# Causal attention in pairs of heads: the last 64 keys of two q-tiles transposed as one block

## The chip, the cores and the metric

The kernel runs on one core of one Trainium2 chip. The metric is the device time of one execution in microseconds (us); of several runs the median counts.

## What is computed

Attention over 2 batches of 12 heads, 448 queries and keys of 64 numbers each, with a causal mask, and behind it two gated layers on the 896 tokens of width 768. All inputs are float32.

```
scores = q @ k.T / 8;  scores[key > query] = -1e9
attn   = exp(scores - rowmax);  attn /= attn.sum() + 1e-9
x      = (attn @ v), heads put side by side          # 896 x 768
x      = (sigmoid(x @ w_gate) * (x @ w_val)) @ w_out  # 768 -> 1536 -> 768
h      = x @ w_in
out    = (h * cos(h)) @ w_out2                        # 768 -> 2048 -> 768
```

## The kernel before

**Tiling.** Two heads of one batch make a pair; there are 12 pairs (t = 0 to 11). The 448 queries are cut into seven q-tiles of 64; the two heads of a pair stand one above the other, so that a q-tile fills 128 partitions. Under the causal mask q-tile i needs 64*(i+1) keys, so its row of probabilities is that wide: 64, 128, ... 448 columns. All seven rows of a pair lie in one buffer `pbuf` (three of them, in turn), at the columns `POFF`; a row with an odd number of 64s (i = 0, 2, 4, 6) has 64 zeros behind it, set once at the start, so that it can be cut into blocks of 128 keys.

**Stages of a pair.** `scores(t)` (L263) makes, tile by tile in the order `ORDER`, the products with the keys on TensorE (PE, L276), the row maximum on VectorE (DVE, L280), and exp with the row's sum on ScalarE (ACT, L284). `normalise(t)` (L255) adds 1e-9 to the sums on GpSimd (POOL, L257), takes the reciprocals on DVE (L258), and multiplies each row in place, rows 0 to 6 one after the other, on POOL (L261). `transposes(t)` (L292) turns 16 blocks of 128x128 on PE (L300), four to a PSUM bank, and copies the banks to `pt`, banks 0 and 2 on DVE (L306), banks 1 and 3 on ACT (L304). `attend(t)` (L309) multiplies with the values (L316): four key blocks j, and for each the q-tiles that need it, one matmul for each head; all fall on one bank. `split_x` takes the result out as a high part (ACT, L328) and a low one (DVE, L330).

**Order.** The schedule is written by hand: every engine runs its instructions in program order. An iteration t of the loop holds `scores(t)`, the loads for later pairs (on SP's queue), `attend(t - 2)`, and `transposes(t - 1)`. Inside the transposes, ahead of the copy of bank 3, stands `normalise(t)`: its reciprocal is queued on DVE behind the copy of bank 2, and the POOL rows of pair t follow that reciprocal. The pair t = 0 alone is normalised in three pieces (`FIRST_ROWS`). From t = 3 on, one step of the preparation of the first weights (`prepare`, lines L137 to L158, on ACT or DVE) stands at the end of each `scores(t)`.

**After attention.** The layers behind it are 2448 matmuls of 448 columns (L209 to L211), with weights that DVE and ACT decode from 64-bit words. The first fifteen and three more of them stand between `transposes(10)`, `attend(10)`, `transposes(11)` and `attend(11)`.

The blocks of the transposes are listed as (q-tile, key block of 128):

```
POFF = [0, 128, 256, 512, 768, 1152, 1536]
BLOCKS = (
    [(i, 0) for i in range(7)] + [(6, 3)]
    + [(i, 1) for i in range(2, 7)] + [(i, 2) for i in range(4, 7)]
)
```

Of the kernel before, what the change touches and what calls it, by code (L numbers as in the profile page):

```python
# [9 lines left out]
F32 = mybir.dt.float32  # L10
# [4 lines left out]
ALU = mybir.AluOpType  # L15
PSUM = bass.MemoryType.PSUM

P = 128
B, H, S, D = 2, 12, 448, 64
NPAIR = H // 2  # L20
# [12 lines left out]
WARM = 26  # L33


POFF = [0, 128, 256, 512, 768, 1152, 1536]
PW = 2048

BLOCKS = (
    [(i, 0) for i in range(7)] + [(6, 3)]  # L40
    + [(i, 1) for i in range(2, 7)] + [(i, 2) for i in range(4, 7)]
)

# [4 lines left out]
VOFF = NQT * QKW  # L50

FIRST_LOADS = ((0, 2), (2, 4), (4, 7))
ATW = VOFF + 4 * P

INV2PI = 1.0 / (2.0 * math.pi)

# [5 lines left out]
def attn_moe_moe2(  # L62
# [9 lines left out]
    nc = tc.nc  # L72
# [8 lines left out]
    def bank():  # L81
        return psum.tile([P, 512], F32, tag="ps", name="ps")
# [14 lines left out]
    for m in range(KX):  # L97
        for c in range(0, KG, WC):
            n = min(WC, KG - c)
# [114 lines left out]
    with tc.tile_pool(name="apool", bufs=1) as apool, tc.tile_pool(name="a2", bufs=2) as a2:  # L214
        ident = apool.tile([P, P], F32, name="ident")
        mask = apool.tile([P, S], F32, name="mask")
        pbuf = [apool.tile([P, PW], F32, name=f"pbuf{i}") for i in range(3)]

# [8 lines left out]
        def load_v(t):  # L227
            vs[t] = a2.tile([P, ATW - VOFF], F32, tag="v", name="v", bufs=4)
            nc.sync.dma_start(out=vs[t], in_=qkv[t, :, VOFF:])
# [15 lines left out]
                compare_op=ALU.is_ge, fill=-8.0e9, base=0, pattern=[[-1, D]], channel_multiplier=1,  # L245
            )
        make_identity(nc, ident)
        for pb in pbuf:
            for i in (0, 2, 4, 6):
                w = D * (i + 1)  # L250
                nc.gpsimd.memset(pb[:, POFF[i] + w : POFF[i] + w + D], 0.0)

        pts, soft = {}, {}

        def normalise(t, i0, i1):  # L255
            pb, (sums, rs) = pbuf[t % 3], soft[t]
            nc.gpsimd.tensor_scalar(sums[:, i0:i1], sums[:, i0:i1], 1e-9, 1.0, op0=ALU.add, op1=ALU.mult)  # L257
            nc.vector.reciprocal(rs[:, i0:i1], sums[:, i0:i1])  # L258
            for i in range(i0, i1):
                row = pb[:, POFF[i] : POFF[i] + D * (i + 1)]  # L260
                nc.gpsimd.tensor_scalar(row, row, rs[:, i : i + 1], 1.0, op0=ALU.mult, op1=ALU.mult)  # L261

        def scores(t):  # L263

            blocks = qk.pop(t).rearrange("p (n c) -> p n c", c=QKW)
            pb = pbuf[t % 3]
            nm = a2.tile([P, 8], F32, tag="nm", name="nm")
            sums = a2.tile([P, 8], F32, tag="sums", name="sums")
            soft[t] = sums, a2.tile([P, 8], F32, tag="rs", name="rs")
            for n, i in enumerate(ORDER):  # L270
                w = D * (i + 1)
                ps = bank()
                for h in range(2):
                    rows = slice(h * D, h * D + D)
                    o, k0 = ((1 - h) * D, 2 * D) if i in CROSSED else (h * D, D)
                    mm(  # L276
                        ps[o : o + D, :w], lhsT=blocks[rows, i, :D],
                        rhs=blocks[rows, : i + 1, k0 : k0 + D], start=True, stop=True,
                    )
                nc.vector.tensor_tensor_reduce(  # L280
                    out=ps[:, :w], in0=ps[:, :w], in1=mask[:, S - w :], scale=-0.125, scalar=3.0e38,
                    op0=ALU.add, op1=ALU.min, accum_out=nm[:, i : i + 1],
                )
                nc.scalar.activation(  # L284
                    pb[:, POFF[i] : POFF[i] + w], ps[:, :w], AF.Exp, scale=-1.0,
                    bias=nm[:, i : i + 1], accum_out=sums[:, i : i + 1],
                )
                if (t, n) in FIRST_ROWS:
                    normalise(0, *FIRST_ROWS[t, n])
            next(preparing, None)  # L290

        def transposes(t, before=lambda g: None):  # L292
            pb = pbuf[t % 3]
            pt = a2.tile([P, 16, P], F32, tag="pt", name="pt")
            for g in range(4):
                ps = bank()
                for s in range(4):
                    i, j = BLOCKS[4 * g + s]
                    c = POFF[i] + j * P
                    nc.tensor.transpose(ps[:, s * P : s * P + P], pb[:, c : c + P], ident)  # L300
                before(g)
                dst = pt[:, 4 * g : 4 * g + 4].rearrange("p a b -> p (a b)")
                if g % 2:
                    nc.scalar.copy(dst, ps)  # L304
                else:
                    nc.vector.tensor_copy(dst, ps)  # L306
            pts[t] = pt

        def attend(t):  # L309

            v, pt = vs.pop(t), pts.pop(t)
            ps = bank()
            for j, (s0, s1) in ((0, (0, 7)), (3, (7, 8)), (2, (13, 16)), (1, (8, 13))):
                for h in range(2):
                    v0 = j * P + h * D
                    mm(  # L316
                        ps[h * D : h * D + D, j * P : S],
                        lhsT=v[:, v0 : v0 + D],
                        rhs=pt[:, s0:s1, h * D : h * D + D],
                        start=j == 0, stop=j == 1,  # L320
                    )
            xps[t] = ps

# [137 lines left out]
    for m in range(KX):  # L461
        ps2 = [bank(), bank()]
        for c in range(nch):
# [4 lines left out]
            for b in range(B):  # L468
                products(ps2[b], wt, HG[c * WC : min(KG, c * WC + WC)], b, c == 0, c == nch - 1)
                if c == nch - 1:  # L470
                    o = tpool.tile([P, S], F32, tag="t0", name="o")
                    rows, c0 = slice(m * P, m * P + P), b * S
# [12 lines left out]
def _layouts(inputs):  # L485
    import numpy as np

    f = np.float32
    q = inputs["q"].reshape(B, NPAIR, 2, NQT, D, D)
    k = inputs["k"].reshape(B, NPAIR, 2, S, D)  # L490
    v = inputs["v"].reshape(B, NPAIR, 2, S, D)
    pk = np.zeros((B, NPAIR, P, ATW), f)
    kt = k.transpose(0, 1, 2, 4, 3)
    qt = q.transpose(0, 1, 2, 5, 3, 4).copy()
    for i in CROSSED:
        qt[:, :, :, :, i] = qt[:, :, ::-1, :, i].copy()
    vb = np.zeros((B, NPAIR, 4 * P, 2, D), f)
    vb[:, :, :S] = v.transpose(0, 1, 3, 2, 4)
    qk = pk[..., :VOFF].reshape(B, NPAIR, P, NQT, 3, D)
    for n, part in enumerate((qt, kt, kt[:, :, ::-1])):  # L500
        qk[..., n, :] = part.reshape(B, NPAIR, P, NQT, D)
    pk[..., :VOFF] = qk.reshape(B, NPAIR, P, VOFF)
    pk[..., VOFF:] = vb.reshape(B, NPAIR, 4, P, P).transpose(0, 1, 3, 2, 4).reshape(B, NPAIR, P, 4 * P)

    def blocks(w):
        w = np.ascontiguousarray(w).view(np.int64)
        kk, nn = w.shape
        return w.reshape(kk // P, P, nn // P, P).transpose(2, 1, 0, 3)

    gv = np.stack([blocks(inputs["moe_w_gate"]), blocks(inputs["moe_w_val"])], axis=2)  # L510
    return {
        "qkv": pk.reshape(B * NPAIR, P, ATW),
        "w_gv": gv,
        "w_out": blocks(inputs["moe_w_out"]),
        "w_in2": blocks(inputs["moe2_w_in"]),
        "w_out2": blocks(inputs["moe2_w_out"]),
    }
# [20 lines left out]
```

## Time and profile before

| | us |
|---|---|
| median of 3 runs (lowest, highest) | 585.95 (585.24, 587.32) |
| the profiled execution, its own time | 587.1 |
| span of the profiled execution | 585.0 |
| PE busy in the span | 578.9 (99%) |
| DVE busy | 377.1 (64%) |
| ACT busy | 273.3 (47%) |
| POOL busy | 45.7 (8%) |
| chain that ended last: PE / POOL | 98% / 1% |

The profile is of one execution; its span goes from the first to the last instruction and is 2.1 us shorter than that execution's own time. PE counts as busy from the start of a matmul to its modelled end, so that 99% does not say that it never waited; the chain of work that ended last, followed back from the last instruction, says more. POOL works in the first 75 us only. Attention takes the span up to about 79 us, with the layers' first products set in at its end.

### The profile page before, as it was taken

Reading aid. Unit: us, or ns where it says so; the run is one execution under the profiler, and the core shown is the slowest. Engines: PE = TensorE matmul, PEld = TensorE weight load, DVE = VectorE, ACT = ScalarE, POOL = GpSimd, SP = SyncE. Lnnn points to the kernel's source line nnn. Section 1 sums busy time; section 2 is a strip of 40 time slices with the busy share of each in tenths; the row PEclk is TensorE's granted clock in tenths of the full one; section 3 lists DMA queues with packets and bytes.
Section 4 is the critical chain, followed back from the end, with each engine's and each line's share of the span. In section 5 each row is a group of like instructions: output and inputs, shape, how many; then the busy total and the mean of one; then the engine's idle time right before and its main releaser. Section 6 shows DMA issues by size and latency. Waiting matters only on the chain.

```text
span 585.0 us, 8308 instructions
## 1 busy us (share of the span) xinstructions
PE 578.9 (99%) x3194; PEld 507.5 (87%) x3194; DVE 377.1 (64%) x659; ACT 273.3 (47%) x549; POOL 45.7 (8%) x119
## 2 busy tenths in 40 slices
PE   8999999999999999999999999999999999999997
PEld 5666789999999999999999999999999999999996
DVE  5899976666666666675555547888888866434620
ACT  6889753333333333332222228777777733312320
POOL 5656610000000000000000000000000000000000
PEclk9999999999999999999999999999999999999999
DMA  7755233333333333333333332333332334433300
GB/s 269 253 193 186 103 108 109 108 109 109 108 109 108 109 108 109 108 108 110 108 109 96 110 101 72 109 109 109 108 109 91 109 105 160 127 132 104 110 32 31
DMA packets 15734, 68.16 MB, mean 117 GB/s; under 512 B 1744, under 2 KB 3664, under 8 KB 15696
## 3 DMA queue, kind: packets, MB, share of 16 engines
q1 hardware_dynamic: 15408, 67.33, 35.5%
q8 instruction: 25, 0.41, 0.3%
q10 hardware_dynamic: 288, 0.31, 0.2%
q14 instruction: 13, 0.11, 0.1%
HBM read 64.88 MB, written 2.75 MB: 116 GB/s over the span
## 4 chain that ended last, share of the span: by engine, by line
PE 98%; POOL 1%; DVE 0%; issue 0%; ACT 0%; ACTq 0%
PE ps L210 29%; PE ps L209 29%; PE ps L211 29%; PE ps L316 4%; PE ps L300 4%; PE ps L276 3%; POOL pbuf L261 1%; PE ps L236 1%; DVE ps L280 0%; POOL sums L257 0%; DVE rs L258 0%; DVE o L476 0%; ACT o L475 0%; DVE nm L280 0%; DVE idle L233 0%
## 5 line engine op out<-in xcount | busy, mean ns | idle before, releaser
L209 PE MATMUL ps<-x,whi 128*128 128x448 f32 x480 | 176.9, 369 | 0.0
L210 PE MATMUL ps<-x,whi 128*128 128x448 f32 x480 | 176.6, 368 | 0.0
L211 PE MATMUL ps<-x,wlo 128*128 128x448 f32 x480 | 176.6, 368 | 0.0
L158 DVE TENSOR_TENSOR wlo<-wf,whi 128x768 fp32r<-128x768 f32 (+2 forms) x71 | 66.0, 930 | 94.6 <-ACT whi L156 92.5
L209 PE MATMUL ps<-h,whi 128*128 128x448 f32 x336 | 123.6, 368 | 0.0
L210 PE MATMUL ps<-h,whi 128*128 128x448 f32 x336 | 123.6, 368 | 0.0
L211 PE MATMUL ps<-h,wlo 128*128 128x448 f32 x336 | 123.6, 368 | 0.0
L209 PEld LDWEIGHTS ps<-x,whi 128*128 128x128 f32 x480 | 90.1, 188 | 9.5 <-issue 0.5
L210 PEld LDWEIGHTS ps<-x,whi 128*128 128x128 f32 x480 | 90.1, 188 | 9.1
L211 PEld LDWEIGHTS ps<-x,wlo 128*128 128x128 f32 x480 | 90.1, 188 | 9.0
L156 ACT ACTIVATE whi<-wf 128x768 fp32r<-128x768 f32 (+2 forms) x71 | 57.6, 812 | 42.7 <-DVE wf L147 42.7
L209 PEld LDWEIGHTS ps<-h,whi 128*128 128x128 f32 x336 | 63.1, 188 | 6.5
L211 PEld LDWEIGHTS ps<-h,wlo 128*128 128x128 f32 x336 | 63.1, 188 | 6.3
L210 PEld LDWEIGHTS ps<-h,whi 128*128 128x128 f32 x336 | 63.1, 188 | 6.3
L147 DVE SCALAR_TENSOR_TENSOR wf<-wraw,wf 128x768 uint32<-128x768 uint32 (+2 forms) x71 | 66.2, 932 | 2.4
L143 DVE SCALAR_TENSOR_TENSOR wf<-wraw,wf 128x768 uint32<-128x768 uint32 (+2 forms) x71 | 66.1, 931 | 2.4
L137 ACT ACTIVATE wf<-wraw 128x768 f32<-128x768 f32 (+2 forms) x71 | 61.8, 870 | 0.0
L385 ACT ACTIVATE h<-pr 128x448 fp32r<-128x448 f32 x24 | 13.9, 578 | 65.2 <-DVE pr L408 61.9
L284 ACT ACTIVATE pbuf<-ps,nm 128x64 f32<-128x64 f32 (+6 forms) x84 | 38.7, 479 | 8.5 <-DVE nm L280 7.5
L261 POOL TENSOR_SCALAR pbuf<-pbuf,rs 128x64 f32<-128x64 f32 (+6 forms) x84 | 40.1, 501 | 14.2 <-PE ps L276 9.2
L139 DVE TENSOR_SCALAR wf<-wf 128x768 uint32<-128x768 uint32 (+1 forms) x70 | 38.2, 546 | 1.3 <-ACT wf L137 0.7
L280 DVE CUSTOM_DVE_ANT_0 ps<-ps,mask 128x64 f32<-128x64 f32 (+6 forms) x84 | 32.9, 454 | 4.8 <-PE ps L276 4.6
(44 smaller groups left out, 404.3 us busy)
## 6 DMA issues: line engine op xcount, KB each, us to landing
wraw<-in_w_gv_dram SPq DMA_DIRECT2D x24, 768.0 KB, 4.3
wraw<-in_w_out_dram SPq DMA_DIRECT2D x24, 768.0 KB, 4.3
wraw<-in_w_in_dram SPq DMA_DIRECT2D x16, 768.0 KB, 4.3
qk<-in_qkv_dram SPq DMA_DIRECT2D x11, 672.0 KB, 4.2
v<-in_qkv_dram SPq DMA_DIRECT2D x12, 256.0 KB, 4.5
wraw<-in_w_out_dram SPq DMA_DIRECT2D x6, 512.0 KB, 3.8
out_dram<-o SPq DMA_DIRECT2D x11, 224.0 KB, 2.0
qk<-in_qkv_dram SPq DMA_DIRECT2D x1, 288.0 KB, 3.5
```

The source lines that it names most:

```text
L137: nc.scalar.activation(w, high.bitcast(F32), AF.Copy, scale=2.0**-112)
L139: nc.vector.tensor_scalar(bits, bits, 3, 0x7FFFFFFF, op0=ALU.logical_shift_left, op1=ALU.bitwise_and)
L143: nc.vector.scalar_tensor_tensor(bits, high, 0x80000000, bits, op0=ALU.bitwise_and, op1=ALU.bitwise_or)
L147: nc.vector.scalar_tensor_tensor(bits, low, 29, bits, op0=ALU.logical_shift_right, op1=ALU.bitwise_or)
L156: nc.scalar.activation(self.hi[:, e0:e1], self.w[:, e0:e1], AF.Copy)
L158: nc.vector.tensor_tensor(self.lo[:, e0:e1], self.w[:, e0:e1], self.hi.bitcast(F32)[:, e0:e1], op=ALU.subtract)
L209: mm(ps[:, :S], lhsT=hi[:, blk], rhs=r[:, 0, cols], start=first and k == 0, stop=False)
L210: mm(ps[:, :S], lhsT=hi[:, blk], rhs=r[:, 1, cols], start=False, stop=False)
L211: mm(ps[:, :S], lhsT=lo[:, blk], rhs=r[:, 0, cols], start=False, stop=last and k == n - 1)
L261: nc.gpsimd.tensor_scalar(row, row, rs[:, i : i + 1], 1.0, op0=ALU.mult, op1=ALU.mult)
L280: nc.vector.tensor_tensor_reduce(out=ps[:, :w], in0=ps[:, :w], in1=mask[:, S - w :], scale=-0.125, scalar=3.0e38, op0=ALU.add, op1=ALU.min ...
L284: nc.scalar.activation(pb[:, POFF[i] : POFF[i] + w], ps[:, :w], AF.Exp, scale=-1.0, bias=nm[:, i : i + 1], accum_out=sums[:, i : i + 1],)
```

## The change

The row of q-tile i no longer has zeros behind it. The half block that an odd row leaves over (its last 64 keys) is transposed together with that of another row: those of q-tiles 2 and 0 as one block, those of 6 and 4 as another. For that the rows stand in `pbuf` in another order: row 2 ends where row 0 begins, and behind row 6 there are 64 columns into which `normalise` writes the last 64 columns of row 4 (its first 256 stay in place). So POOL multiplies row 4 in two instructions, of 256 and of 64 columns. The memsets of the zeros are gone.

Of the 16 blocks 14 are left: six with j = 0 (q-tiles 1 to 6), the two mixed ones, four with j = 1, two with j = 2. The fourth bank holds two blocks, and its copy on ACT has 256 columns.

In `attend` a mixed block has two sorts of keys above each other, so the values come in seven blocks of 128 rows instead of four: three full ones, and four in which 64 rows are values and 64 are zeros. `VALUES` lists (values block, first slot, last slot, first q-tile); there are seven products for each head instead of four, over the same 16 tiles of 64 columns. The load of the values of a pair grows from 256 to 448 KB.

```diff
-POFF = [0, 128, 256, 512, 768, 1152, 1536]
-PW = 2048
+POFF = [192, 256, 0, 384, 1024, 640, 1344]
+APART = {4: 1792}
+HALF = {2: 128, 6: 1728}
+PW = 1856
 BLOCKS = (
-    [(i, 0) for i in range(7)] + [(6, 3)]
-    + [(i, 1) for i in range(2, 7)] + [(i, 2) for i in range(4, 7)]
+    [(i, 0) for i in range(1, 7)] + [(2, None), (6, None)]
+    + [(i, 1) for i in range(3, 7)] + [(i, 2) for i in (5, 6)]
 )
+VALUES = ((3, 6, 7, 0), (0, 0, 6, 1), (4, 6, 7, 2), (5, 7, 8, 4), (6, 7, 8, 6), (1, 8, 12, 3), (2, 12, 14, 5))
-ATW = VOFF + 4 * P
+NVB = 7
+ATW = VOFF + NVB * P
...
-        for pb in pbuf:
-            for i in (0, 2, 4, 6):
-                w = D * (i + 1)
-                nc.gpsimd.memset(pb[:, POFF[i] + w : POFF[i] + w + D], 0.0)
...
             for i in range(i0, i1):
-                row = pb[:, POFF[i] : POFF[i] + D * (i + 1)]
-                nc.gpsimd.tensor_scalar(row, row, rs[:, i : i + 1], 1.0, op0=ALU.mult, op1=ALU.mult)
+                c, w = POFF[i], D * (i + 1)
+                moves = [(c, c, w)]
+                if i in APART:
+                    moves = [(c, c, w - D), (APART[i], c + w - D, D)]
+                for c0, c1, w in moves:
+                    nc.gpsimd.tensor_scalar(
+                        pb[:, c0 : c0 + w], pb[:, c1 : c1 + w], rs[:, i : i + 1], 1.0,
+                        op0=ALU.mult, op1=ALU.mult,
+                    )
...
-                for s in range(4):
-                    i, j = BLOCKS[4 * g + s]
-                    c = POFF[i] + j * P
+                part = BLOCKS[4 * g : 4 * g + 4]
+                for s, (i, j) in enumerate(part):
+                    c = HALF[i] if j is None else POFF[i] + j * P
                     nc.tensor.transpose(ps[:, s * P : s * P + P], pb[:, c : c + P], ident)
...
-            for j, (s0, s1) in ((0, (0, 7)), (3, (7, 8)), (2, (13, 16)), (1, (8, 13))):
+            for j, s0, s1, i in VALUES:
                 for h in range(2):
                     v0 = j * P + h * D
                     mm(
-                        ps[h * D : h * D + D, j * P : S],
+                        ps[h * D : h * D + D, i * D : i * D + (s1 - s0) * D],
                         lhsT=v[:, v0 : v0 + D],
                         rhs=pt[:, s0:s1, h * D : h * D + D],
-                        start=j == 0, stop=j == 1,
+                        start=j in (0, 3), stop=j in (2, 3),
                     )
```

On PE, at the end of iteration 4 (`attend(2)`, then the transposes of pair 3), there stands before, with the waits of each row in brackets (Pool_49 is a wait for POOL):

```order
L316 MATMUL ps<-pt,v 64x448 [waits DMAHW2_49,DVE_49]
L316 MATMUL ps<-pt,v 64x448
L316 MATMUL ps<-pt,v 64x64 x2
L316 MATMUL ps<-pt,v 64x192 x2
L316 MATMUL ps<-pt,v 64x320 x2
L300 MATMUL ps<-ident,pbuf_83 128x128 [waits Activation_49,Pool_49]
L300 MATMUL ps<-ident,pbuf_83 128x128 [waits Pool_49] x3
L300 MATMUL ps<-ident,pbuf_83 128x128 [waits Activation_49,Pool_49]
L300 MATMUL ps<-ident,pbuf_83 128x128 [waits Pool_49] x2
L300 MATMUL ps<-ident,pbuf_83 128x128
```

and now:

```order
L328 MATMUL ps<-pt,v 64x384 x2
L328 MATMUL ps<-pt,v 64x64 x6
L328 MATMUL ps<-pt,v 64x256 x2
L328 MATMUL ps<-pt,v 64x128 x2
L311 MATMUL ps<-ident,pbuf_83 128x128 [waits Activation_49,Pool_49]
L311 MATMUL ps<-ident,pbuf_83 128x128 [waits Pool_49] x3
L311 MATMUL ps<-ident,pbuf_83 128x128 [waits Activation_49,Pool_49]
L311 MATMUL ps<-ident,pbuf_83 128x128 [waits Pool_49]
L311 MATMUL ps<-ident,pbuf_83 128x128 x2
```

The last transpose that waits for POOL, the first block of row 6, was the seventh of the pair and is now the sixth.

On POOL, `normalise` of one pair stands before as

```order
L257 TENSOR_SCALAR sums<-sums 128x7 [waits Activation_49,Pool_49]
L261 TENSOR_SCALAR pbuf_85<-pbuf_85,rs 128x64 [waits DVE_49,PE_49]
L261 TENSOR_SCALAR pbuf_85<-pbuf_85,rs 128x128
L261 TENSOR_SCALAR pbuf_85<-pbuf_85,rs 128x192 [waits PE_49]
L261 TENSOR_SCALAR pbuf_85<-pbuf_85,rs 128x256 [waits PE_49]
L261 TENSOR_SCALAR pbuf_85<-pbuf_85,rs 128x320 [waits PE_49]
L261 TENSOR_SCALAR pbuf_85<-pbuf_85,rs 128x384 [waits PE_49]
L261 TENSOR_SCALAR pbuf_85<-pbuf_85,rs 128x448 [waits PE_49]
```

and now:

```order
L261 TENSOR_SCALAR sums<-sums 128x7 [waits Activation_49,Pool_49]
L269 TENSOR_SCALAR pbuf_85<-pbuf_85,rs 128x64 [waits DVE_49,PE_49]
L269 TENSOR_SCALAR pbuf_85<-pbuf_85,rs 128x128
L269 TENSOR_SCALAR pbuf_85<-pbuf_85,rs 128x192
L269 TENSOR_SCALAR pbuf_85<-pbuf_85,rs 128x256 [waits PE_49] x2
L269 TENSOR_SCALAR pbuf_85<-pbuf_85,rs 128x64
L269 TENSOR_SCALAR pbuf_85<-pbuf_85,rs 128x384 [waits PE_49]
L269 TENSOR_SCALAR pbuf_85<-pbuf_85,rs 128x448 [waits PE_49]
```

Row 4, of 320 columns, has become one of 256 and one of 64, ahead of rows 5 and 6.

## Rows read from the trace of the kernel before

**Rows 1.** Windows: busy us (x instructions) of each engine; PE clock; DMA share.
```profile
12.65:16.00 3.35, 3.35 (x33) 2.21 (x31) 2.50 (x11) 2.73 (x11) 2.58 (x7) 0.50 0.72 289
18.30:67.60 49.30, 49.30 (x542) 32.70 (x540) 45.46 (x169) 43.86 (x156) 30.34 (x72) 1.00 0.61 212
```
**Rows 2.** The chain, one pair: start us, us, engine, line.
```profile
40.30 1.90 PE ps L300 x16
42.20 1.67 PE ps L276 x22
43.87 1.88 PE ps L316 x16
45.76 1.90 PE ps L300 x16
```
**Rows 3.** The chain: the transposes of pairs 1 and 10.
```profile
18.32 1.90 PE ps L300 x16
...
67.74 1.90 PE ps L300 x16
```
**Rows 4.** Timeline of the same pair: start us, us, engine, line [idle before <-releaser].
```profile
42.41 0.19 DVE L258 RECIPROCAL rs<-sums 128x7 f32<-128x7 f32 x1
42.77 3.20 POOL L261 TENSOR_SCALAR pbuf<-pbuf,rs 128x64 f32<-128x64 f32 x7 [1.17 <-PE ps L276]
45.64 0.73 DVE L143 SCALAR_TENSOR_TENSOR wf<-wraw,wf 128x384 uint32<-128x384 uint32 x1
45.69 1.97 PE L300 MATMUL ps<-ident,pbuf 128*128 128x128 f32 x16
46.38 0.69 DVE L306 COPY pt<-ps 128x512 f32<-128x512 f32 x1
...
47.25 0.69 DVE L306 COPY pt<-ps 128x512 f32<-128x512 f32 x1 [0.18 <-PE ps L300]
47.86 0.19 DVE L258 RECIPROCAL rs<-sums 128x7 f32<-128x7 f32 x1
```
**Rows 5.** Groups by shape, the shortest products with the values: count, busy us, mean ns.
```profile
L316 PE MATMUL ps<-pt,v 128*64 128x64 f32 x48 | 3.4, 220 | 0.0
```
**Rows 6.** Groups by shape, POOL from 42.7 to 46 us.
```profile
L261 POOL TENSOR_SCALAR pbuf<-pbuf,rs 128x448 f32<-128x448 f32 x1 | 0.6, 643 | 0.0
...
L261 POOL TENSOR_SCALAR pbuf<-pbuf,rs 128x320 f32<-128x320 f32 x1 | 0.5, 535 | 0.0
L261 POOL TENSOR_SCALAR pbuf<-pbuf,rs 128x256 f32<-128x256 f32 x1 | 0.5, 483 | 0.0
...
L261 POOL TENSOR_SCALAR pbuf<-pbuf,rs 128x64 f32<-128x64 f32 x1 | 0.3, 319 | 1.2 <-PE ps L276 1.2
```
**Rows 7.** Groups by shape, DVE's decoding steps, whole span.
```profile
L143 DVE SCALAR_TENSOR_TENSOR wf<-wraw,wf 128x768 uint32<-128x768 uint32 x63 | 60.5, 961 | 2.2
...
L143 DVE SCALAR_TENSOR_TENSOR wf<-wraw,wf 128x512 uint32<-128x512 uint32 x6 | 4.2, 692 | 0.2
...
L143 DVE SCALAR_TENSOR_TENSOR wf<-wraw,wf 128x384 uint32<-128x384 uint32 x2 | 1.5, 730 | 0.0
```
**Rows 8.** The chain at the start, up to the end of the first transposes.
```profile
9.02 0.98 POOL pbuf L261 x2
...
10.58 1.21 POOL pbuf L261 x2
...
11.83 1.69 PE ps L300 x10
```
**Rows 9.** Timeline of the last pair's normalising, POOL and DVE.
```profile
70.20 4.90 POOL L261 TENSOR_SCALAR pbuf<-pbuf,rs 128x64 f32<-128x64 f32 x7 [1.21 <-DVE rs L258]
...
72.86 1.17 DVE L147 SCALAR_TENSOR_TENSOR wf<-wraw,wf 128x768 uint32<-128x768 uint32 x1
```
**Rows 10.** Waits from 69 to 77 us: who for whom, us, times, longest.
```profile
PEld ps L300 <- POOL pbuf L261: 0.5, 1, 0.5
```
**Rows 11.** DMA issues of the page: count, KB each, us to landing.
```profile
v<-in_qkv_dram SPq DMA_DIRECT2D x12, 256.0 KB, 4.5
```

More of the change, by code (lines that the diff above doesn't have):

```diff
@@ L33 @@
 WARM = 26
-POFF = [0, 128, 256, 512, 768, 1152, 1536]
-PW = 2048
+POFF = [192, 256, 0, 384, 1024, 640, 1344]
+APART = {4: 1792}
+HALF = {2: 128, 6: 1728}
+PW = 1856
 BLOCKS = (
-    [(i, 0) for i in range(7)] + [(6, 3)]
-    + [(i, 1) for i in range(2, 7)] + [(i, 2) for i in range(4, 7)]
-)
+    [(i, 0) for i in range(1, 7)] + [(2, None), (6, None)]
+    + [(i, 1) for i in range(3, 7)] + [(i, 2) for i in (5, 6)]
+)
+HALVES = (0, 2, 4, 6)
+VALUES = ((3, 6, 7, 0), (0, 0, 6, 1), (4, 6, 7, 2), (5, 7, 8, 4), (6, 7, 8, 6), (1, 8, 12, 3), (2, 12, 14, 5))
 CROSSED = (2, 4, 5)
@@ L293, in transposes @@
             pb = pbuf[t % 3]
-            pt = a2.tile([P, 16, P], F32, tag="pt", name="pt")
+            pt = a2.tile([P, len(BLOCKS), P], F32, tag="pt", name="pt")
             for g in range(4):
                 ps = bank()
-                for s in range(4):
-                    i, j = BLOCKS[4 * g + s]
-                    c = POFF[i] + j * P
+                part = BLOCKS[4 * g : 4 * g + 4]
+                for s, (i, j) in enumerate(part):
+                    c = HALF[i] if j is None else POFF[i] + j * P
                     nc.tensor.transpose(ps[:, s * P : s * P + P], pb[:, c : c + P], ident)
                 before(g)
-                dst = pt[:, 4 * g : 4 * g + 4].rearrange("p a b -> p (a b)")
+                dst = pt[:, 4 * g : 4 * g + len(part)].rearrange("p a b -> p (a b)")
+                src = ps[:, : len(part) * P]
                 if g % 2:
-                    nc.scalar.copy(dst, ps)
+                    nc.scalar.copy(dst, src)
                 else:
-                    nc.vector.tensor_copy(dst, ps)
+                    nc.vector.tensor_copy(dst, src)
             pts[t] = pt
@@ L496, in _layouts @@
         qt[:, :, :, :, i] = qt[:, :, ::-1, :, i].copy()
-    vb = np.zeros((B, NPAIR, 4 * P, 2, D), f)
-    vb[:, :, :S] = v.transpose(0, 1, 3, 2, 4)
+    vb = np.zeros((B, NPAIR, NVB, P, 2, D), f)
+    vt = v.transpose(0, 1, 3, 2, 4)
+    vb[:, :, :3] = vt[:, :, : 3 * P].reshape(B, NPAIR, 3, P, 2, D)
+    for n, i in enumerate(HALVES):
+        o = (n + 1) % 2 * D
+        vb[:, :, 3 + n, o : o + D] = vt[:, :, i * D : i * D + D]
     qk = pk[..., :VOFF].reshape(B, NPAIR, P, NQT, 3, D)
@@ L502, in _layouts @@
     pk[..., :VOFF] = qk.reshape(B, NPAIR, P, VOFF)
-    pk[..., VOFF:] = vb.reshape(B, NPAIR, 4, P, P).transpose(0, 1, 3, 2, 4).reshape(B, NPAIR, P, 4 * P)
+    pk[..., VOFF:] = vb.reshape(B, NPAIR, NVB, P, P).transpose(0, 1, 3, 2, 4).reshape(B, NPAIR, P, NVB * P)
     def blocks(w):
```

## The prediction

> **What bounds the kernel now.** I read the windows first, then the chain, then the timeline of one pair. The windows say that from 18.30 to 67.60 PE is busy all the time at the full clock (granted 1.00, the level of 2.4 GHz), and that DVE is busy for 45.46 of these 49.30 us [rows 1]. The chain there is PE alone: transposes 1.90, scores 1.67, values 1.88, and the next pair's transposes begin 5.46 us after the last [rows 2]. So a pair costs what PE's instructions cost, and an instruction less on PE is worth its time as long as nobody else becomes late. Behind attention the chain is PE's layer products, which the change leaves alone. What I look for is who is next, and the timeline gives that.
>
> One loop goes round once a pair through four engines [rows 4]: the reciprocal R on DVE (42.41) releases POOL's rows (42.77, that is R + 0.36; they take 3.20 and end at 45.97); the last of them, row 6, is needed by the seventh transpose; after the twelfth transpose DVE copies bank 2 (47.25), and behind that copy stands the next reciprocal (47.86). How much room has it? The sixteen transposes start at 45.69; the last starts 0.27 (the mean of their own length, 1.97 less 1.70) before their end, so fifteen steps take 1.70: 0.06 for the first, whose weights could not be loaded beside earlier work, and 0.109 each. The weights of one are loaded while the one before runs, so row 6 is wanted at 45.69 + 0.06 + 5 x 0.109 = 46.29. It is there at 45.97, and PE goes on about 0.05 after POOL's end where it does wait (10.58 + 1.21 = 11.79 and 11.83 in [rows 8]). The room is 0.27 us.
>
> **The transposes: two fewer for each pair.** 2 x 0.109 = 0.22 off PE, on its path: 1.90 becomes 1.68. The twelfth transpose, which sets the loop going, stays the twelfth.
>
> **The values: seven products instead of four.** The columns stay: 16 tiles of 64, for two heads, and fp32 makes two passes of each. Price of a cut: a 64-column product is four instructions a pair (two heads side by side, two passes), 3.4 us / 12 = 0.28 in all, with 0.220 for one, so the second pass starts 0.06 behind the first [rows 5]; the average over all tiles is 1.88 / 32 = 0.059. Short passes thus cost little more than their columns. Six more passes: 0 at the low end (the columns are the same), 6 x 0.220 = 1.3 us a pair at the high end, if none overlapped. I take 0.02, near the low end, since the row just read is of exactly this shape. PE's pair: 1.67 + 1.90 + 1.68 = 5.25.
>
> **POOL: one instruction more.** Row 4 was 535 ns and is now 483 + 319 [rows 6]. Rows overlap a little: the seven by their own lengths sum to 3.38 and take 3.20, so 0.03 at each joint. Added: 0.483 + 0.319 - 0.535 - 0.03 = 0.24 us, ahead of row 6.
>
> **The loop after the change.** Three things eat the room of 0.27: PE's pair shorter by 0.20, row 6 wanted one transpose earlier (0.11), POOL longer by 0.24. Together 0.55; PE now waits, about 0.28 at the sixth transpose of each pair. The loop from reciprocal to reciprocal: 0.36 + 3.44 (POOL) + 0.05 = R + 3.85 for the weights of row 6; 0.06 + 6 x 0.109 = 0.71 to the start of the twelfth transpose; 0.30 from there to the copy (45.69 + 0.06 + 11 x 0.109 = 46.95, copy at 47.25); 0.61 from the copy to the next reciprocal. Sum **5.47**. I take that for the pair: what PE saves, it spends in waiting for POOL.
>
> **DVE.** In seven of the pairs its queue holds, ahead of the copies, a step of the weights' preparation. It starts at R + 3.23 and is not done before row 6 is: 45.64 to 46.37, which is 0.40 after POOL's end [rows 4]. The 384-wide step takes 730 ns there, against 961 for 768 and 692 for 512 columns elsewhere, which makes about 0.56 for 384 alone (an estimate from these two) [rows 7]. So the two engines exclude each other here. With row 6 ending at R + 3.80 the step ends at R + 4.20, the two copies follow 0.61 apart, the reciprocal comes 0.61 behind the second: 5.42, just inside the loop's 5.47. Those 0.05 are all that hides this edit; were they gone, the pair would grow by what is missing.
>
> The Trainium skill, SBUF — State Buffer, section "Who interferes with whom", says that VectorE and GpSimd share a port pair as an exclusive lock: a DVE instruction with two SBUF inputs and a GpSimd one that reads SBUF shut each other out, and whoever issues first keeps it for the whole instruction. The trace agrees, with the 0.40 behind POOL's end. By it the sum stays as it is while row 6 issues first, and becomes the second rival's if DVE does.
>
> **ACT, DMA, memsets.** ACT's copy of bank 3 is half as wide; ACT is busy 43.86 of 49.30 and not on the chain, so this is worth nothing by itself. But the steps from pair 1 to pair 10 average (67.74 - 18.32) / 9 = 5.49 [rows 3], 0.03 above the pair of rows 2; PE's new idle time would take up such delays. The values' loads grow by 192 KB; each lands 4.5 us after its issue now [rows 11] and is used two pairs, 11 us, later; at a DMA share of 0.61 the queue has room, so even half as long again changes nothing. If that cover were gone, PE would wait for the load's remainder. The twelve memsets stood before any POOL work on the chain: nothing.
>
> **The start.** Pair 0's rows are on the chain: rows 3 and 4 (9.02), sums, reciprocal, rows 5 and 6 (10.58), PE at 11.83 [rows 8]. All behind row 4 moves by 0.24; nine transposes instead of ten are left behind row 6. But the clock falls to the half level (1.2 GHz; granted 0.50 from 12.65 to 16.00 [rows 1]), and the later ones cost twice: from 12.07 about five fit before the fall and four come after it, so the stretch again takes about 1.7, and its end is 0.24 late. Of a delay that lies in the half-clock stretch half is made good when the clock returns at the same time: +0.12, with the values +0.14. Bounds: 0 and +0.26.
>
> **The end.** Pair 11 is normalised while DVE decodes weights, so its rows take 4.90, up to 75.10 [rows 9], and PE waits for them already [rows 10]. Row 4's second piece adds 0.24, one transpose fewer behind row 6 takes 0.11 off, the values add 0.02: +0.15.
>
> **The sum.** Nine steps: 9 x 5.47 - 49.42 = -0.19. Start +0.14, end +0.15. Together **+0.1 us** on a span of 585.0, or on the 587.1 of that execution. That execution is 1.15 above the median of the runs, 585.95, so I forecast 586.05, rounded 586.1: no change that can be measured. (About 0.3%, 1.8 us, is what a measurement here can tell from none.)
>
> **Rival 1: PE's saving arrives.** If POOL did not hold PE (rows faster than I add up, or row 6 not wanted so early), a pair would cost PE's 5.25: 9 x 5.25 - 49.42 = -2.2, with start and end +0.3 at most: about 584.0, faster by 0.3%. Against it: every term of the loop is a measured row, and 0.28 must be wrong. Chance 0.09.
>
> **Rival 2: DVE comes between rows 5 and 6 (slower).** Row 6 (643 ns [rows 6]) starts at 45.97 - 0.64 = 45.33 now, 0.31 before the preparation step at 45.64 [rows 4]; then it starts at R + 3.80 - 0.64 = R + 3.16, the step at R + 3.23, so the lead is 0.07. If DVE got in first, its step would run to R + 3.79 and row 6 after it. A 448-wide row that was shut out needs about 0.51 more: at the end of the last pair, after DVE's step ends at 74.03, rows 5 and 6 take 1.07, of which 0.61 is row 6, so 0.46 for 384 columns [rows 9]; that gives R + 4.30. The loop: 4.30 + 0.05 + 0.71 + 0.30 + 0.61 = 5.97, +0.50 in each of seven pairs, +3.5: **589.6**. It decides where the lead goes below zero. For it: 0.07 is thin, and a row starts before its forerunner has ended. Against it: POOL is still first. Chance 0.13.
>
> **Rival 3: short passes don't overlap.** At the high end of the values' price a pair grows by 1.3 less the 0.22 of waiting that it replaces, +10 us in all: 596. Against it the row of 64 columns. Or the clock stays at the half level longer at the start, +1.5. Together 0.04.
>
> **That the change does not do what it says** cannot be: the order shows 14 transposes.
>
> **Chances.** The forecast 0.74, which with the start's and the end's bounds and the spread of the runs (585.24 to 587.32) covers 584.6 to 587.6. To leave out no more than 2 in 10 the range goes up towards the second rival, as fewer than seven pairs may be hit: 584.6 to 588.6. Faster 0.09, same 0.74, slower 0.17.
>
> **What would show it.** In the changed profile: transposes x14 with a wait of their weight loads for POOL in each pair, ending at POOL's last row; pairs 5.47 apart; the 384-wide steps of DVE at about 0.97 instead of 0.73 (0.56 and a last POOL row above 1 us would be rival 2); products with the values at 1.90. I am wrong if pairs are 5.25 apart, or if POOL's rows take other than 3.44.

## The result and the profile after

The changed kernel takes **577.54 us** (median of 4; 577.28 to 577.99), the kernel before beside it 585.7 (4 runs, 585.24 to 587.32): a ratio of 0.9857, interval 0.9836 to 0.9877. All four executions before are of the kind with the longer step described below; the other kind, which makes up 20 of the 74 executions of that kernel on record, takes 575.2 to 577.6 us, and the changed kernel is not faster than those. The forecast was 586.1, no change, in a range that began at 584.6. The profiled execution took 577.28, its span is 575.1; before it was 587.1 and 585.0. The medians lie 8.2 apart and the profiled executions 9.8, because a fall of PE's clock at the start (last section) is in all four executions after, and by its time in one of the four before, the 587.32 (the profiled execution, 587.1, has it too).

The windows of both kernels, four stretches of 120 us of the layers' products (columns as in [rows 1]), before:

```profile
90.00:210.00 120.00, 120.00 (x582) 109.01 (x581) 73.37 (x97) 42.54 (x64) 0.00 (x0) 1.00 0.35 109
210.00:330.00 120.00, 120.00 (x582) 108.99 (x581) 67.89 (x89) 38.91 (x57) 0.00 (x0) 1.00 0.35 107
330.00:450.00 120.00, 120.00 (x583) 108.99 (x582) 98.00 (x146) 80.77 (x143) 0.00 (x0) 1.00 0.31 103
450.00:570.00 120.00, 120.00 (x582) 109.01 (x581) 65.25 (x90) 41.98 (x67) 0.00 (x0) 1.00 0.33 108
```

and the same windows after:

```profile
90.00:210.00 120.00, 120.00 (x594) 111.20 (x593) 75.27 (x100) 44.62 (x67) 0.00 (x0) 1.00 0.34 109
210.00:330.00 120.00, 120.00 (x594) 111.19 (x593) 69.96 (x91) 38.92 (x56) 0.00 (x0) 1.00 0.34 106
330.00:450.00 120.00, 120.00 (x594) 111.20 (x593) 99.34 (x150) 81.77 (x147) 0.00 (x0) 1.00 0.31 103
450.00:570.00 120.00, 120.00 (x594) 111.20 (x593) 59.96 (x83) 38.14 (x60) 0.00 (x0) 1.00 0.34 107
```

PE counts as busy throughout in both, its granted clock is 1.00 in both, and still one makes 582 products in 120 us and the other 594. By the starts of the products in the trace the step from one to the next is 206.67 ns before (207, 207, 206, over and over) and 202.67 ns after (207, 203, 202, 203, 199). Both hold for the whole run of 2430 products, whose instructions are the same in both kernels, and neither cares how busy the others are: DVE works 98.00 us of one stretch and 65.25 of another, and the count stays 582 or 583. 2430 x 4.0 ns = **9.7 us**: the whole gain. I call the two the long and the short step (the expectations below say the slow and the fast pace). In each of the 20 profiled executions these 2430 products keep to one of them, or, where a product was put in between, have the same one ahead of it and behind it; by their times, executions of the same kernel differ in it.

The timelines where the long run begins (start us, us, engine, line), before:

```profile
78.52 0.44 PE L316 MATMUL ps<-pt,v 128*64 128x320 f32 x2
78.89 0.47 PE L209 MATMUL ps<-x,whi 128*128 128x448 f32 x1
79.20 0.36 PE L210 MATMUL ps<-x,whi 128*128 128x448 f32 x1
79.40 0.37 PE L211 MATMUL ps<-x,wlo 128*128 128x448 f32 x1
79.61 0.37 PE L209 MATMUL ps<-x,whi 128*128 128x448 f32 x1
```

and after:

```profile
78.43 0.38 PE L328 MATMUL ps<-pt,v 128*64 128x128 f32 x3
78.74 0.47 PE L218 MATMUL ps<-x,whi 128*128 128x448 f32 x1
79.05 0.36 PE L219 MATMUL ps<-x,whi 128*128 128x448 f32 x1
```

The run begins at 78.89 before and at 78.74 after. So attention, the object of the whole prediction, came out 0.15 us apart, which is luck in part (next section but one). In it the loop that I had worked out is there. One pair after, in the timeline, for [rows 4] (from 41.5 to 47.6 us):

```profile
42.04 0.19 DVE L262 RECIPROCAL rs<-sums 128x7 f32<-128x7 f32 x1
42.40 3.43 POOL L269 TENSOR_SCALAR pbuf<-pbuf,rs 128x64 f32<-128x64 f32 x8 [1.19 <-DVE rs L262]
45.13 1.96 PE L311 MATMUL ps<-ident,pbuf 128*128 128x128 f32 x14
45.27 0.96 DVE L152 SCALAR_TENSOR_TENSOR wf<-wraw,wf 128x384 uint32<-128x384 uint32 x1
45.88 0.96 PEld L311 LDWEIGHTS ps<-ident,pbuf 128*128 128x128 f32 x9 [0.23 <-POOL pbuf L269]
47.52 0.19 DVE L262 RECIPROCAL rs<-sums 128x7 f32<-128x7 f32 x1
```

PEld stands for PE's weight loads. The sixth of them waits for POOL and starts 0.05 behind its end (42.40 + 3.43 = 45.83; 45.88); the next reciprocal comes 5.48 behind the last. What went beside the forecast shows in the chain of pair 2 (start us, us, engine, line), for [rows 2]:

```profile
23.16 1.81 PE ps L311 x14
24.98 2.11 PE ps L287 x22
27.09 1.91 PE ps L328 x28
```

The scores, 1.67 in an undisturbed pair, took 2.11 there.

### The profile page after: what moved, and what is told of

It reads as the page before. It is cut to its first block, busy times and chain, and to the rows that moved or that the text cites. A ratio compares the mean times of both kernels' runs of the same rounds, so it can differ in the third digit from the quotient of the medians.

```text
span 575.1 us, 8548 instructions
## 1 busy us (share of the span) xinstructions
PE 568.2 (99%) x3314; PEld 508.8 (88%) x3314; DVE 377.6 (66%) x659; ACT 268.6 (47%) x549; POOL 47.4 (8%) x119
## 4 chain that ended last, share of the span: by engine, by line
PE 97%; POOL 2%; DVE 1%; issue 0%; POOLq 0%; ACT 0%; ACTq 0%; DVEq 0%
PE ps L218 29%; PE ps L219 29%; PE ps L220 29%; PE ps L328 4%; PE ps L311 4%; PE ps L287 3%; POOL pbuf L269 1%; PE ps L245 1%; DVE ps L291 0%; DVE pt L318 0%; DVE rs L262 0%; POOL sums L261 0%; DVE o L488 0%; ACT o L487 0%; DVE nm L291 0%
## 5 line engine op out<-in xcount | busy, mean ns | idle before, releaser
L269 POOL TENSOR_SCALAR pbuf<-pbuf,rs 128x64 f32<-128x64 f32 (+3 forms) x96 | 42.9, 469 | 15.2 <-DVE rs L262 15.2
```

The lines of the kernel that those rows point to most:

```text
L269: nc.gpsimd.tensor_scalar(pb[:, c0 : c0 + w], pb[:, c1 : c1 + w], rs[:, i : i + 1], 1.0, op0=ALU.mult, op1=ALU.mult,)
```

## The experiments

**Two theories** on the long step. R: an execution draws it by chance, whatever the kernel. E: something in how PE enters the long run sets it, and the kernel decides how likely that is. (The first expectations call E theory A, and theory B there is that the place in PE's instruction stream does it.) The first experiments ask for E where the entry differs: the last of the products with the values has 320 columns before and 128 after.

**Another last product in the kernel before.** For pair 11 alone the 64-column product goes last.

```
-            for j, (s0, s1) in ((0, (0, 7)), (3, (7, 8)), (2, (13, 16)), (1, (8, 13))):
+            last = 3 if t == NP - 1 else 1
+            for j, (s0, s1) in sorted((...), key=lambda e: e[0] == last):
```

> The kernel before; only in the last pair's attend the order of the four key blocks is 0, 2, 1, 3, so that a 64-column product and not a 320-column one stands last ahead of the long run of layer products. Same instructions, same addresses, same count. Theory A (how PE enters the long run decides its pace): the pace can leave 206.67 ns and become 202.67, and then the time is about 576 to 578; it need not do so with this very width. Theory B (the pace hangs on how many PE instructions stand ahead in the program): 206.67, 585 to 587.

Measured: 575.87 and 575.82, beside two long ones in seven executions of the kernel before. Again on another chip, where the kernel before had the long step in 11 of 11 executions:

> The kernel before with a 64-column product last ahead of the long run, as in b_last64, more executions. Theory R: slow pace (585 to 587) in about as many executions as the kernel before beside it. Theory E: none, all at 575.7 to 577.2.

575.72, 575.8, 575.44, 575.57; ratio to before 0.9825 (0.9808 to 0.9842). One reordered product, no work saved, and the kernel before is as fast as the changed one. R falls: 0 of 4 against 11 of 11 on one chip.

**A disturbance in the middle.** One unused product of 64 columns stands 1152 products before the end of the run of the kernel before.

```
+        if f == 0:
+            mm(bank()[:, :D], lhsT=wt[0][:, :P], rhs=X[0][:, 0, :D], start=True, stop=True)
```

> The kernel before with one extra product of 64 columns, whose result is not used, in the midst of the long run: ahead of the first product of the third layer stage, with 1152 products still to come. Theory A (pace is a state of PE's queue that any disturbance may reset): 206.67 ns up to there, and 202.67 behind it if the state flips, 4.6 us less, about 581; if it doesn't flip, 586. Theory B: two more PE instructions, also either; but then b_warm30 must be able to flip it too. A slower operand address or a slower neighbour as the cause would leave 206.67 on both sides.

> The kernel before with one extra 64-column product 1152 products ahead of the end, more executions. If a disturbance ahead of a product sets the pace anew: executions that enter slow end at about 580.5 to 581 (slow up to there, 202.67 behind it), those that enter fast at 575.8 or 577.2, and, if it can also turn a fast run slow, some at 580.5 from that side; none at 585 or more. If the pace can't be reset within the run: 576 or 585.5 only, as the kernel before, and the 580.49 seen once stays unexplained.

Measured: 575.78, 580.49; then 575.86, 580.72, 581.36, 580.46, 582.44, 581.04. Two began with the short step; six began with the long one and came in 4 to 5 us under the kernel before (585.4 there, and 587.0 to 587.4 with the clock's fall, to which the 582.44 belongs): 1152 x 4 ns = 4.6. No execution was left at 585. So, by the times, the step is held by the flow of the products itself, and a single short product in it lets the long one go. No trace shows the turn, as both profiled executions began with the short step.

**More products at the very start** (`WARM` 30 for 26).

> The kernel before with 30 instead of 26 warming matmuls at the very start: eight more PE instructions ahead of everything, entry of the long run untouched. Theory A (entry): 206.67 ns, 585 to 587. Theory B (place in the instruction stream): the pace may change to 202.67, about 577.

587.21 and 575.71: both occur, as in the kernel before. Two executions can't show that the odds are the same, but eight instructions more ahead of the run don't take the long step away.

**The changed kernel again, and with 256 columns last** (in `VALUES` the product of block 1 goes last for pair 11).

> The changed kernel unaltered, several executions beside as many of the kernel before on one chip, to see how often either shows which pace of the layer products (206.67 or 202.67 ns a product, some 9.8 us over the run) and whether the clock falls at the start (about 1.5 us). Theory R (each execution draws its pace, the kernel has no part in it; so far the kernel before had the slow one in about half of its executions): two or more of six at 585 to 587, and at the same pace and the same start the two kernels agree within 0.5 us. Theory E (the last products ahead of the run set the odds; 128 columns wide here, 320 before): none of six above 578, while the kernel before still shows 585 to 587 in some.

> The changed kernel with the order of the last pair's value products altered so that one of 256 columns, not of 128, stands last ahead of the long run. Theory R: slow pace in about as many executions as the kernel before. Theory E with width as the cause: the slow pace (585 to 587) appears in some executions, as it does with 320 columns. Theory E with something else at the entry as the cause: none.

576.65, 576.5, 577.29, 577.82; and 576.45, 577.53, 578.42, 575.86. Short step in all, beside 11 of 11 long ones of the kernel before.

**Is it the width?** An unused pair of products of 320 or of 64 columns goes right ahead of the run, in the changed kernel and in the kernel before (`n` = 5 or 1):

```
             xps[t] = ps
+            if t == NP - 1:
+                extra = bank()
+                for h in range(2):
+                    mm(extra[h * D : h * D + D, : n * D], lhsT=v[:, P + h * D : P + h * D + D],
+                       rhs=pt[:, 8 : 8 + n, h * D : h * D + D], start=True, stop=True)
```

> The changed kernel with one more pair of products with the values (both heads, 320 columns, the keys of block 1, into a bank that nobody reads) as the last instructions ahead of the layers' long run; the extra work costs some 0.54 us. Theory E, that the last product ahead of the run sets the run's pace and that 320 columns there set the slow one: pace 206.7 ns a product in most executions, hence 577.5 + 0.5 + 2430 x 0.004 = about 587.7 us, and 578 in the rest. Rival W, that the width of the last product is not what does it (something else of the kernel before does): pace 202.7 ns, 578.0 us in all executions.

> The same, with 64 columns in the extra pair of products instead of 320; it costs some 0.11 us. Theory E: pace 202.7 ns, 577.0 to 577.8 us in all executions. If it were the extra product itself that sets the slow pace, whatever its width: 587 us.

> The kernel before with an unused pair of products of 320 columns (keys of block 1, into a bank of its own) right ahead of the long run, +0.54 us. If 320 columns as the last product set the slow pace given the rest of the kernel before: 586 us in most executions, as before. If it is the order of the PSUM banks (the extra bank turns it by one for all products behind it) that keeps the fast pace: 576.3 us in all.

> The same with 64 columns, +0.11 us. By the theory that a short last product keeps the fast pace, and also by the one of the banks: 575.9 us in all executions. If only what stands ahead of the last product matters: 585.6 in most.

a_extra320: 577.04 to 578.83 (4); a_extra64: 576.36 to 578.36 (4); b_extra320: 575.69 to 577.88 (10); b_extra64: 575.71 to 577.55 (10). All short. My form of E, that a 320-column product in the last place sets the long step, fell: in b_extra320 the very operands of the last product of the kernel before stand there once more. The extra bank also turns the order of the PSUM banks by one, so that was taken alone, with a product of zeros at the start:

```
+        mm(bank()[:, :D], lhsT=idle, rhs=idle[:, :D], start=True, stop=True)
```

> The kernel before with one more product of 64 columns (of zeros, into a bank of its own) at the very start, behind the zeros that are multiplied there, +0.1 us at most: it turns the order of the PSUM banks by one everywhere and leaves the entry into the long run as it is. If the order of the banks sets the pace: 575.8 in all executions. If the entry does: 585.5 in most, as before.

575.77 to 586.86: five of ten long. The banks are not it either. Then 320 columns last in the changed kernel without added work, and the kernel before with 192 and 64 columns in exchanged places ahead of its last product:

```
+LAST_VALUES = ((3, 6, 7, 0), (0, 0, 1, 1), (4, 6, 7, 2), (1, 8, 12, 3), (5, 7, 8, 4), (6, 7, 8, 6), (2, 12, 14, 5),
+    (0, 1, 6, 2))
```

> The changed kernel, where for the last pair alone the product of 384 columns is cut into one of 64 and one of 320 columns and the one of 320 comes last, straight ahead of the layers' long run, behind one of 128 columns; no work is added, no PSUM bank is moved. If a last product of 320 columns is enough for the slow pace (206.7 ns a product): some 587 us in most executions. If not, as the unused products of 320 columns suggested: 202.7 ns, 576.4 to 578 us in all.

```
+            order = (0, 2, 3, 1) if t == NP - 1 else (0, 3, 2, 1)
```

> The kernel before, where for the last pair alone the product of 192 columns changes places with the one of 64, so that the last is still that of 320 columns, on the same operands and bank, and only what stands ahead of it differs (448, 192, 64, 320 instead of 448, 64, 192, 320 columns). If the last product is what gives the slow pace its chance: 585.5 us in about two of three executions, as before. If the row of the last few products does it (their time pattern): 575.8 us in all, or another share of slow ones.

a_last320_b: 578.18, 577.96, 578.44, 576.28, all short. b_order: 584.97 to 587.0, long in 11 of 11. The entry of b_order in the timeline (start us, us, engine, line):

```profile
76.77 0.71 PE L317 MATMUL ps<-pt,v 128*64 128x320 f32 x4
77.41 0.47 PE L209 MATMUL ps<-x,whi 128*128 128x448 f32 x1
77.73 0.36 PE L210 MATMUL ps<-x,whi 128*128 128x448 f32 x1
```

and that of a_last320_b:

```profile
79.02 0.71 PE L332 MATMUL ps<-pt,v 128*64 128x320 f32 x4
79.66 0.47 PE L221 MATMUL ps<-x,whi 128*128 128x448 f32 x1
79.97 0.36 PE L222 MATMUL ps<-x,whi 128*128 128x448 f32 x1
```

These rows differ in one thing: from the first product to the second it takes 0.32 in the one and 0.31 in the other. In the trace's nanoseconds it is 313 in all profiled executions with the long step (before, b_warm30, b_order) and 306 to 310 in all with the short one. These few nanoseconds go with the step; whether they set it or only show it is open. All executions together, told apart by their times (long: 584.8 to 587.4 us; short: 574.1 to 578.8; b_kick as above), the profiled ones by the step as well:

| kernel | last products before the run, columns | executions | long step |
|---|---|---|---|
| before, in six sessions | 448, 64, 192, 320 | 74 | 54 |
| b_bank, b_warm30 | the same | 12 | 6 |
| b_kick, b_kick_more (at the entry) | the same | 8 | 6 |
| b_order | 448, 192, 64, 320 | 11 | 11 |
| b_last64, b_last64_more | 448, 192, 320, 64 | 6 | 0 |
| b_extra64, b_extra320 | those of before, and 64 or 320 unused | 20 | 0 |
| after, a_again, a_same, a_act, a_best, a_best_more | ..., 256, 128 | 26 | 0 |
| a_last256, a_last320_b | ..., 128, 256 or 320 | 8 | 0 |
| a_extra64, a_extra320 | ..., 128, and 64 or 320 unused | 8 | 0 |

By session the kernel before had the long step in 4 of 4, 2 of 7, 11 of 11, 8 of 11, 15 of 26 and 14 of 15 executions; the others ran beside these.

So E holds in its wide form: by kernel, what stands at the entry sets how often the long step comes (77 of 105 executions in the upper four lines, none of 68 in the lower five). This is shown for the kernel before, whose variants differ from it there alone, but for the turn of the banks that was tried by itself. Within that kernel the executions still differ, and what draws the step in one of them is not known. That the entry also gives the changed kernel its short step is argued from this and not shown, for no variant of it brought the long one. What in the entry of the kernel before does it stays open: not the width of the last product, its operands, the banks or, as far as eight instructions show, the place in the stream, each by itself.

**The attention part: POOL and ACT.** First, row 4's 64 columns are multiplied on ACT instead of POOL (pair 0: on DVE).

```
...
+        def apart(t):
+            for i, c in APART.items():
+                s, r = POFF[i] + D * i, soft[t][1][:, i : i + 1]
+                nc.scalar.activation(pbuf[t % 3][:, c : c + D], pbuf[t % 3][:, s : s + D], AF.Copy, scale=r)
...
```

> The changed kernel, with the second piece of row 4 (64 columns) taken from POOL and given to ACT, behind its copy of bank 3 (for pair 0 to DVE). The loop through POOL loses 0.29 us: 5.18 a pair, and PE's own 5.25 to 5.30 binds instead of 5.47. Theory of the prediction (POOL's loop holds the pairs): pairs 5.25 to 5.30 apart, 1.5 to 2.0 us less attention than the changed kernel, 575.5 to 576. If POOL's loop is not what holds PE: 5.47, 577.5. The pace of the layer products may flip as well, which the profile shows apart: 202.67 expected, since the entry is the same.

575.46, 577.12, 577.0, 576.96. Pairs 1 to 10 took 49.19 (after: 49.55); the steps of 5.47 became 5.26 to 5.41. So POOL did hold those pairs, but only part of the way. What is left shows in the waits of the weight loads in a_act (who for whom, us, times, longest; 16.5 to 65.7 us):

```profile
PEld ps L322 <- POOL pbuf L269: 1.0, 6, 0.2
PEld ps L298 <- ACT x L353: 0.7, 4, 0.2
```

Six times POOL is still waited for, and four times the scores wait 0.2 for ACT's high part of an earlier pair; two of those scores take 1.81 and 1.80 in the chain (at 34.66 and 45.48) instead of 1.67. The two longest steps, 5.84 and 5.80, stayed. In both kernels these pairs have a step of the weight preparation on ACT (so has the pair behind each of them, which is not long: 5.40 and 5.51 in the changed kernel). In the timeline of ACT in the changed kernel (start us, us, engine, line), ahead of the copy of bank 1:

```profile
23.58 0.60 ACT L295 ACTIVATE pbuf<-ps,nm 128x384 f32<-128x384 f32 x1
24.14 0.59 ACT L146 ACTIVATE wf<-wraw 128x384 f32<-128x384 f32 x1
24.59 0.57 ACT L340 ACTIVATE x<-ps 128x448 fp32r<-128x448 f32 x1
25.01 0.90 ACT L316 COPY pt<-ps 128x512 f32<-128x512 f32 x2
```

and the waits there (who for whom, us, times, longest; 24.9 to 27.2 us):

```profile
PEld ps L287 <- ACT pt L316: 0.3, 1, 0.3
PEld ps L287 <- ACT wf L146: 0.2, 1, 0.2
```

The next scores need banks that ACT still has to empty. So ACT's preparation steps were put behind the transposes' copies (DVE's stay where they were), on top of the edit above:

```
-            [(k.decode, 0, a)], [(k.decode, 0, b)], ...
+            [], [(k.decode, 0, a)], [], [(k.decode, 0, b)], ...
+            next(preparing, None)        # behind transposes(t - 1)
```

> The changed kernel with two things done to attention: row 4's last 64 columns are multiplied on ACT instead of POOL (pair 0: on DVE), which alone took the step of a pair from 5.47 to 5.26 to 5.40 us; and the steps of the weight preparation that ACT does stand behind the transposes' copies instead of ahead of them, so that they delay no copy. If the two longer steps of a pair (5.84 and 5.80) come from those steps of ACT: pair 1 to pair 10 in 47.4 to 48.2 us instead of 49.2, and the whole at 574.0 to 575.8 us. If they come from elsewhere: 49.2 us, and 575.5 to 577.0. Pace 202.7 ns a product by theory E, since the last product ahead of the run has 128 columns as in the changed kernel.

> The changed kernel with row 4's second piece on ACT and ACT's preparation steps behind the copies once more, beside the unaltered one on the same chip: 575.0 us where the clock does not fall at the start and 576.2 where it does, 1.5 us under the unaltered one in each case. If the gain over it was the chip's: less than 0.5 us.

> The changed kernel unaltered, beside the others on the same chip: 576.5 us where the clock does not fall at the start, 577.5 where it does, and never the slow pace (that would be 587).

The same place of ACT in a_best_more, in the timeline:

```profile
22.95 0.58 ACT L353 ACTIVATE x<-ps 128x448 fp32r<-128x448 f32 x1
23.37 0.90 ACT L327 COPY pt<-ps 128x512 f32<-128x512 f32 x2
24.30 0.35 ACT L283 ACTIVATE pbuf<-pbuf,rs 128x64 f32<-128x64 f32 x1
24.56 0.55 ACT L146 ACTIVATE wf<-wraw 128x384 f32<-128x384 f32 x1
```

and its chain from those scores on:

```profile
23.65 1.80 PE ps L298 x24
25.45 1.91 PE ps L341 x28
27.36 1.68 PE ps L322 x14
```

Scores 1.80 where they were 2.11; both long pairs became 5.39, and pairs 1 to 10 take 48.27 instead of 49.55 (a_same). I had expected 47.4 to 48.2. Times: a_best 574.96 to 576.37 (6), a_best_more 574.1 to 575.0 (4), a_same beside it 577.36 to 578.38. Where the clock falls at the start (below), 576.0 to 576.4 against a_same's 577.4 to 578.4; where it does not, 574.1 to 575.1 against 576.5 and 576.65 of a_again, on another chip: some 1.5 to 2 us. Its ratio to the kernel before on that chip is 0.9809 (0.9795 to 0.9824), most of which is the step of the products; against executions of the kernel before with the short step, on the earlier chip, it was 0.9997 (0.998 to 1.0013). So it beats the changed kernel, and the kernel before wherever that has the long step; over a kernel before with the short step that ratio shows no gain. The traces hint at one: the nine steps, 48.27, are 1.13 under those of b_last64_more (49.40), and the long run begins at 75.98 (a_best_more) and 76.46 (a_best) against 77.20. Of the times without the clock's fall, a_best's 574.96 and 575.08 stand beside 575.75, 576.07 and 576.13 of the kernel before. That points to about 1 us, from few executions.

## Why the prediction was wrong

**The step that failed** is one clause: behind attention "the chain is PE's layer products, which the change leaves alone". It left alone the instructions, and not their time. 86% of the span was costed at nothing, with no row read from it and no rival placed in it. A hint lay in the trace of before: the first fifteen products, set in behind `transposes(10)`. In the timeline, the first two and the last of them:

```profile
69.39 0.45 PE L209 MATMUL ps<-x,whi 128*128 128x448 f32 x1
69.68 0.37 PE L210 MATMUL ps<-x,whi 128*128 128x448 f32 x1
...
72.31 0.37 PE L211 MATMUL ps<-x,wlo 128*128 128x448 f32 x1
```

From the second to the fifteenth, (72.31 - 69.68) / 13 = 0.202 us each, on the same kind of product that takes 0.207 from 78.89 on, at the same granted clock (1.00 in the window from 69.40 to 72.40). One kind of instruction with two steps in one trace means that the step is not a constant of it.

The Trainium skill, TensorE: Matmul & The Clock Gate, section "Back-to-back issue gap", gives an isolated spacing of N / 2.4 + 2.5 ns, an estimated 189 ns for 448 columns, and says that weight loads and products together set it in a real stream. The trace does not show 189; it shows 202.67 and 206.67, at one clock.

With 9.7 us for the step put back, the profiled execution of after would be 577.28 + 9.7 = 587.0, beside 587.1. Point by point:

- **The transposes and values.** 1.68 and 1.90 a pair were forecast. The chain after has transposes of 1.68 where nothing holds them, and values of 1.91 in each pair. Right: the values grew by 0.03 (from 1.88) for a forecast of 0.02; short passes overlap, and the first half of rival 3 falls.
- **POOL and the loop.** Rows 3.44 forecast, 3.43 measured; reciprocal to reciprocal 5.47 forecast, 5.48 measured; waits in pairs 1 to 10:

```profile
PEld ps L311 <- POOL pbuf L269: 1.4, 7, 0.2
```

  Seven waits of 0.2, forecast 0.28 in each pair. Right where nothing else held the pair, which was three of the nine steps (5.26, 5.84, 5.40, 5.33, 5.47, 5.47, 5.47, 5.80, 5.51). Rival 1 falls.
- **DVE.** 0.97 forecast for the step of 384 columns, 0.96 measured, ending 0.40 behind POOL's end (46.23 and 45.83) as in [rows 4]. POOL kept its lead (row 6 takes 640 ns on the mean of nine pairs, 643 in [rows 6]), and rival 2 falls. The Trainium skill, SBUF — State Buffer, section "Who interferes with whom", has the engine that issued first keep the port; by this row the trace agrees.
- **ACT: the term that was mis-sized.** I had PE's new idle time absorb its delays. It did not: the two pairs with ACT's preparation steps were 5.64 and 5.59 before and are 5.84 and 5.80 now. Nine steps took 49.55 where -0.19 off 49.42 was forecast; the 0.32 between is these two, 0.37 and 0.33 above the loop's 5.47, less 0.38 in the four steps that were not 5.47 otherwise (5.26, 5.40, 5.33, 5.51). a_best took them away. PE's idle time lay at the sixth transpose, ahead of the copies, and the delay behind it, at the scores.
- **Start and end.** The end, right: from `transposes(10)` to the run 11.22 before, 11.36 after: +0.14 for a forecast of +0.15. At the start POOL's piece costs what was worked out (in [rows 8] two rows take 0.98; now three take 1.22):

```profile
8.69 1.22 POOL pbuf L269 x3
...
10.49 1.21 POOL pbuf L269 x2
...
11.74 2.18 PE ps L311 x9
```

  The nine transposes took 2.18 where about 1.7 was forecast: the forecast had the clock fall and return when it did before, but it stands at 0.50 from 12.62 to 16.04 before and from 11.30 to 14.72 after. That is 3.42 us in both, so the second half of rival 3 falls too. And the clock's fall moves the stretch more than the piece does: pair 0 to pair 1 is 9.38 before, 9.24 after and 9.48 in a_same, where it falls, and 7.08 (b_last64_more) and 7.24 (a_again), where it does not.
- **The total of attention was near by luck.** Of the -0.15 between the two profiled executions, the start has -0.42 (the transposes of pair 1 at 18.32 and 17.90 in the chain; +0.14 forecast), the nine steps +0.13 (-0.19 forecast) and the end +0.14. The errors cancel.
- **The sign of the edit in attention.** Where both run with the short step and without the fall, the long run begins at 77.20 (b_last64_more) and at 78.11 (a_again), and the executions take 575.4 to 575.8 and 576.5 to 576.65. Not all of these 0.9 us are the edit's: 0.32 is the first load, behind which the first scores begin at 7.84 in the one and at 8.16 in the other (at 7.96 in a_last256, at 8.05 in b_order, so it differs by execution). From there to the transposes of pair 1 it takes 8.82 and 8.98, +0.16 for a forecast of +0.14; the nine steps take 49.40 and 49.69, +0.29 for -0.19; the end has +0.15 for +0.15. So without the fall the fewer transposes cost some 0.6 us. The forecast of +0.1 had the side and both ends right, and missed ACT in the nine steps.

## What to carry to other kernels

Before a part of the program is costed at nothing because its instructions stay, read its step from two places of the trace, and take several executions of both kernels: here a step of 202.67 or 206.67 ns over 2430 products outweighs all that was won or lost ahead of it. A gain that such a step gives is not owed to the edit's purpose; here one reordered product gives it as well (b_last64). And idle time that an edit makes covers a delay only where it lies behind that delay on the same path.

## What was not expected of the hardware

- A steady stream of weight loads and products of 448 columns keeps one of two steps, 206.67 or 202.67 ns, for 492 to 502 us; an interval of 313 ns or of 306 to 310 ns behind the first product goes with it, and one 64-column product in the stream turns, by the times, the long one into the short one (b_kick_more, 5 of 5 that began long). The mechanism is open.
- The fall of the clock at the start does not come in each execution, and costs 1 to 2 us: 576.5 and 576.65 without it, 577.29 and 577.82 with it (a_again, mean granted clock 1.0 and 0.997); 584.9 to 585.8 and 587.0 to 587.4 for the kernel before beside it.
